# A gated feed-forward layer after linear attention: the last four tiles of w_gate and w_val in blocks 3 to 8 as seven products for eight, and the attention of batches 4 to 7 one to four slots ahead of its old place

## The chip, the cores and the metric

One core of one Trainium2 chip. The metric is device time in microseconds (us); with one core, that core's span is what counts. All runs quoted here are compared with runs of the kernel before on the same chip.

## The reference, cut to what matters

```python
# 8 batches, 8 heads, 576 tokens, head size 64
kv  = einsum('bhsd,bhse->bhde', k, v)
o   = einsum('bhsd,bhde->bhse', q, kv)
o   = o / sqrt(mean(o * o, axis=-1) + 1e-6) * g_norm
x   = o.transpose(0, 2, 1, 3).reshape(4608, 512)
g   = x @ w_gate                       # 512 x 1536
val = x @ w_val                        # 512 x 1536
ffn = (gelu(g) * val) @ w_out          # 1536 x 512
out = x + sigmoid(x @ w_res) * ffn
```

The 4,608 tokens go through in nine blocks of 512, numbered 0 to 8. Blocks 0 to 7 hold the first 512 tokens of batches 0 to 7. Block 8 holds the 64 last tokens ("the remainder") of all eight batches. While the layer runs for block m, the attention of batch m+1 is computed between its tiles.

## The kernel before

A block has slots: 12 tiles of w_gate and w_val (128 hidden units each), then the residual gate, then the product with w_out. A tile costs TensorE (PE) eight matmuls of 512 columns. ScalarE (ACT) takes the gelu and VectorE (DVE) multiplies it by the value, which frees the value's PSUM bank:

```python
pmoe  = tile_pool(name="pmoe",  bufs=4, space=PSUM)     # four banks, tag "mm"
pattn = tile_pool(name="pattn", bufs=4, space=PSUM)     # four banks, tag "at"
# ... cut ...
def m_act(blk, f, gps, vps):
    ge = moep.tile([P, NJ * P], FP16, tag="ge", name="ge")
    nc.scalar.activation(out=ge, in_=gps, func=AF.Gelu)
    nc.vector.tensor_tensor(out=hids[blk][:, f, :], in0=ge, in1=vps, op=ALU.mult)   # "hid"

def m_gval(blk, f, pool=pmoe, tag="mm"):
    # ... cut ...
    gps = pool.tile([P, NJ * P], FP32, tag=tag, name="gps")
    m_mm(gps, wg_c, f, blk, 0, NJ)
    vps = pool.tile([P, NJ * P], FP32, tag=tag, name="vps")
    m_mm(vps, wv_c, f, blk, 0, NJ)
    m_act(blk, f, gps, vps)
```

The attention of the next batch is spread over the slots. Its output "op" fills four "at" banks. ACT squares them, DVE sums the squares ("ss"), DVE works out 1/rms (the norm, 12 small operations), and DVE scales the output ("t"). After that t is multiplied by g ("t-times-g") and transposed by DMA into xT, the next block's input:

```python
def plan_attn(b):
    rem = pair(b) is not None            # batches 2, 3, 5, 7 carry remainder rows
    m = b - 1
    # ... b == 2 cut ...
    at(m - 1, NF, lambda: by_token(b, "q"))                  # NF = 12
    at(m - 1, NF + 1, lambda: by_token(b, "k"), *begin)      # begin: q's transposes by DMA
    k0, o0, n0 = 1, 3, 7
    at(m, k0, lambda: a_kv(b))                               # k-times-v
    if rem:
        at(m, o0 - 1, lambda: a_rem_o(b))                    # remainder's output, "orp"
        at(m, o0 + 2, lambda: a_ss(b, NJ))
    at(m, o0, lambda: a_o(b))                                # attention output, "op"
    for j in range(NJ):
        at(m, o0 + j // 2, lambda j=j: a_ss(b, j))           # sums of squares
    at(m, n0, lambda: a_norm(b, 0, NJ + rem))                # the norm
    n0 += 1 if b == 2 else 2
    for j in range(NJ):
        at(m, ..., lambda j=j: a_t(b, j))                    # scalings "t", slots 9 and 10
    for j in range(NJ):
        at(m, ..., lambda j=j: a_x(b, j))                    # t-times-g
    at(m, NF, lambda: d_xT(b, 0, NJ))                        # the transpose into xT
```

The product with w_out is already computed as seven products for eight in blocks 1 to 8 (the Strassen-Winograd scheme). Four sums of quarters of hid ("hid_s", DVE) feed it, and the operation "wF" frees a bank that it needs soon after its start.

## Time and profile before

| | before |
|---|---|
| time | 344.26 us, median of three runs (344.17 to 344.53) |
| busy | PE 96%, DVE 68%, ACT 43%, GpSimd (POOL) 30% |
| blocks 3 and 5 / 4 and 6 (with remainder) | 34.88 / 35.24 and 35.23 us |
| blocks 7 / 8 (no attention inside) | 33.35 / 32.11 us |
| waits of PE in blocks 3 to 8 | none |

A block's length is the time from its first gate matmul to that of the next block, in PE's timeline; block 8 is measured to the start of its last product group. Engine shares are averages over the whole span. The profiled run of before took 347.15 us, because v came late in its opening (PE waited 2.5 us). Spans of profiled runs are therefore not compared here; lengths of blocks are.

### The profile page before, as it was taken

Reading aid. Unit: us, or ns where it says so; the run is one execution under the profiler, and the core shown is the slowest. Engines: PE = TensorE matmul, PEld = TensorE weight load, DVE = VectorE, ACT = ScalarE, POOL = GpSimd, SP = SyncE. Lnnn points to the kernel's source line nnn. Section 1 sums busy time; section 2 is a strip of 40 time slices with the busy share of each in tenths; the row PEclk is TensorE's granted clock in tenths of the full one; section 3 lists DMA queues with packets and bytes.
Section 4 is the critical chain, followed back from the end, with each engine's and each line's share of the span. In section 5 each row is a group of like instructions: output and inputs, shape, how many; then the busy total and the mean of one; then the engine's idle time right before and its main releaser. Section 6 shows DMA issues by size and latency. Waiting matters only on the chain.

```text
span 345.4 us, 6165 instructions
## 1 busy us (share of the span) xinstructions
PE 331.9 (96%) x2432; PEld 188.0 (54%) x2432; DVE 236.5 (68%) x446; ACT 150.1 (43%) x265; POOL 103.1 (30%) x121
## 2 busy tenths in 40 slices
PE   8789999999899999999999999999999999999992
PEld 3544454445744475447544764476447644764481
DVE  5665549769859987698578976885688735453643
ACT  3573384274336352535263615361736133623350
POOL 2692161980064108200820083005000600050013
PEclk9899999999999999999999999999999999999997
DMA  7999999669589263966395439744003120030004
GB/s 244 290 178 204 195 204 166 168 95 150 117 108 164 94 123 120 165 60 128 130 167 43 102 114 174 79 92 153 17 0 61 63 76 2 1 121 4 0 2 121
DMA packets 76399, 38.81 MB, mean 112 GB/s; under 512 B 42066, under 2 KB 73810, under 8 KB 76370
## 3 DMA queue, kind: packets, MB, share of 16 engines
q0 software_dynamic: 38752, 17.17, 40.1%
q1 hardware_dynamic: 37184, 20.71, 21.6%
q10 hardware_dynamic: 434, 0.52, 0.5%
q8 instruction: 19, 0.31, 0.4%
q14 instruction: 10, 0.08, 0.1%
HBM read 38.80 MB, written 9.44 MB: 140 GB/s over the span
## 4 chain that ended last, share of the span: by engine, by line
PE 69%; DVE 2%; issue 0%; POOL 0%; POOLq 0%; DVEq 0%
PE gps L336 21%; PE vps L336 20%; PE wA L431 10%; PE rps L356 6%; PE wF L431 3%; PE wD L431 2%; PE w L431 2%; PE wE L431 2%; PE kvp L187 1%; PE op L205 1%; DVE t L282 1%; DVE hid L325 1%; DVE hid_s L404 0%; DVE t L296 0%; POOL osb L526 0%
## 5 line engine op out<-in xcount | busy, mean ns | idle before, releaser
L324 ACT ACTIVATE ge<-gps 128x512 f16<-128x512 f32 x108 | 64.3, 597 | 133.1 <-PE gps L336 127.8
L325 DVE TENSOR_TENSOR hid<-ge,vps 128x512 f16<-128x512 f16 x108 | 73.8, 684 | 63.2 <-PE vps L336 60.8
L336 PE MATMUL vps<-xT,wv 128*128 128x512 f16 x424 | 108.8, 379 | 0.4 <-DVE hid L325 0.4
L336 PE MATMUL gps<-xT,wg 128*128 128x512 f16 x424 | 109.0, 379 | 0.0
L470 POOL TENSOR_TENSOR osb<-osb,t 128x512 f32<-128x512 f32 x28 | 36.1, 1309 | 155.6 <-DVE osb L466 148.6
L336 PEld LDWEIGHTS <-wv 128*128 128x128 f16 x424 | 41.5, 98 | 50.6 <-issue 0.7
L336 PEld LDWEIGHTS <-wg 128*128 128x128 f16 x424 | 40.2, 98 | 45.4 <-issue 0.4
L431 PEld LDWEIGHTS <-hid_s 128*128 128x128 f16 x384 | 37.5, 98 | 6.3 <-issue 1.4
L356 PE MATMUL rps<-wr,xT 128*128 128x512 f16 x144 | 32.7, 379 | 0.0
L431 PEld LDWEIGHTS <-hid 128*128 128x128 f16 x288 | 28.2, 98 | 5.1
L365 ACT ACTIVATE th<-rps 128x512 f32<-128x512 f32 x36 | 21.5, 597 | 19.0 <-PE rps L356 19.0
L356 PEld LDWEIGHTS <-xT 128*128 128x128 f16 x144 | 14.1, 98 | 16.8
L224 DVE TENSOR_REDUCE ss<-sq 128x8 f32<-128x512 f32 x32 | 20.6, 679 | 2.9 <-ACT sq L222 2.7
L431 PE MATMUL wA<-wo_ts,hid_s 128*128 128x256 f16 x168 | 20.6, 273 | 1.2 <-DVE wF L404 1.2
L370 ACT ACTIVATE th<-th 128x512 f32<-128x512 f32 x36 | 19.9, 622 | 0.0
L282 DVE TENSOR_TENSOR t<-op,ny 128x512 f16<-128x512 f32 x28 | 17.9, 682 | 0.1
L222 ACT ACTIVATE sq<-op 128x512 f32<-128x512 f32 x28 | 15.3, 597 | 4.5 <-PE op L205 4.2
L296 DVE TENSOR_TENSOR t<-t,g 128x512 f16<-128x512 f16 x36 | 16.2, 498 | 0.1
L404 DVE TENSOR_TENSOR hid_s<-hid 128x1536 f16<-128x1536 f16 x16 | 15.3, 955 | 0.3
L526 POOL TENSOR_TENSOR osb<-osb,t 128x512 f32<-128x512 f32 (+1 forms) x4 | 4.3, 1078 | 27.8 <-DVE osb L522 27.8
L373 PE MATMUL fps<-wo,hid 128*128 128x512 f16 x48 | 11.2, 379 | 0.0
L431 PE MATMUL wD<-wo_ts,hid_s 128*128 128x256 f16 x84 | 10.3, 273 | 0.1
(133 smaller groups left out, 326.5 us busy)
## 6 DMA issues: line engine op xcount, KB each, us to landing
out_dram<-osb SPq DMA_DIRECT2D x14, 512.0 KB, 2.6
qraw<-in_q_dram POOLq DMA_DIRECT2D x7, 512.0 KB, 8.2
kraw<-in_k_dram POOLq DMA_DIRECT2D x7, 512.0 KB, 9.9
v<-in_v_dram POOLq DMA_DIRECT2D x7, 512.0 KB, 11.9
out_dram<-osb SPq DMA_DIRECT2D x5, 256.0 KB, 2.8
wg<-in_moe_w_gate_dram POOLq DMA_DIRECT2D x2, 512.0 KB, 9.2
wv<-in_moe_w_val_dram POOLq DMA_DIRECT2D x2, 512.0 KB, 9.4
wo<-in_moe_w_out_dram POOLq DMA_DIRECT2D x2, 512.0 KB, 14.2
```

The costliest lines, as they stand in the source:

```text
L222: nc.scalar.activation(out=sq, in_=src, func=AF.Square)
L224: nc.vector.tensor_reduce(out=out_, in_=sq, op=ALU.add, axis=mybir.AxisListType.X)
L282: nc.vector.tensor_tensor(out=t, in0=o, in1=scale, op=ALU.mult)
L296: nc.vector.tensor_tensor(out=t_t[blk][:, jj, :], in0=t_t[blk][:, jj, :], in1=g16, op=ALU.mult)
L324: nc.scalar.activation(out=ge, in_=gps, func=AF.Gelu)
L325: nc.vector.tensor_tensor(out=hids[blk][:, f, :], in0=ge, in1=vps, op=ALU.mult)
L336: nc.tensor.matmul(ps[:, j0 * P : j1 * P], lhsT=w[:, cc, :], rhs=xT_t[blk][:, j0:j1, cc, :], start=(cc == 0 and j0 == 0), stop=(cc == NP - ...
L356: nc.tensor.matmul(rps, lhsT=xT_t[blk][:, j, cc, :], rhs=wr16[:, cc, :], start=(cc == 0), stop=(cc == NP - 1),)
L365: nc.scalar.activation(out=th, in_=rps, func=AF.Tanh, scale=0.5)
L370: nc.scalar.activation(out=th, in_=th, func=AF.Copy, scale=0.5, bias=0.5)
L431: nc.tensor.matmul(ps[:, e - es[0], :], lhsT=a[:, f, e * P : (e + 1) * P], rhs=b[:, f, :], start=(start and e == es[0] and f == 0), stop=( ...
L470: nc.gpsimd.tensor_tensor(out=res_all[of], in0=res_all[of], in1=t_t[blk][of], op=ALU.add)
```

## The change

The intent is to take columns off PE, which is the busiest engine. For the last four of the 12 tiles in blocks 3 to 8, w_gate and w_val are split into halves of the contraction and of the hidden units, x into halves of the contraction and of the tokens. Seven products of quarters then give what eight did. In exchange there are sums of x (GpSimd), sums of weights (DVE, once), copies (ACT) and additions (DVE). The second part moves the attention of batches 4 to 7 ahead (the output by one slot, the norm by three, the scalings by four), so that it is through DVE before the products begin. Batch 3's attention keeps its slots, but the reordering and transposing of its q and k go later, behind block 1's output.

```diff
+    def gval_by_products(blk):
+        w = [{}, {}]                        # two groups g of 128 hidden units
+        # prod_w: gate and value side by side in one bank, 4 matmuls of 256 columns
+        def first():
+            for g in range(2):
+                w[g]["E"] = pmoe.tile([P, 2, PR], FP32, tag="mm", name="gE")
+                w[g]["D"] = pmoe.tile([P, 2, PR], FP32, tag="mm", name="gD")
+                w[g]["A"] = pattn.tile([P, 2, PR], FP32, tag="at", name="gA")
+                w[g]["d"] = th_all[:, g, :].rearrange("p (n t) -> p n t", n=2)
+                prod_w(w[g]["A"], g, wh(1, 1), x_of(blk, 1, 1), True)
+                nc.scalar.copy(out=w[g]["E"], in_=w[g]["A"])
+            for g in range(2):
+                prod_w(w[g]["D"], g, s_(1), x_sum[:, 0], True)
+                nc.scalar.copy(out=w[g]["d"], in_=w[g]["D"])
+        def second():
+            for g in range(2):
+                prod_w(w[g]["A"], g, s_(2), x_sum[:, 1], False)
+                sub(nc.vector, w[g]["D"], w[g]["A"], w[g]["d"], ALU.add)
+            for g in range(2):
+                prod_w(w[g]["E"], g, wh(1, 2), x_of(blk, 2, 1), False)
+                gelu(g, "C11", w[g]["E"], F0, 0)
+            times(0, "C11")
+        # third(), fourth(): three more products, half gelus and half products; cut
...
             if b == 3:
+                plans[m - 1][NF + 3] = [by_token k, by_token q, *begin] + ...   # behind block 1's output
+            else: # as before
-            k0, o0, n0 = 1, 3, 7
+            k0, o0, n0 = (1, 3, 7) if b == 3 else (0, 2, 4)
...
-        n0 += 1 if b == 2 else 2
+        n0 += 1 if b != 3 else 2                        # scalings in slots 5 and 6
...
-            at(m, NF if b == 2 else n0 + 1, lambda j=j: a_x(b, j))
+            at(m, n0 + 1 if b == 3 else NF, lambda j=j: a_x(b, j))
...
+            plan[10] = [lambda: w_sums(0), lambda: w_sums(1)]       # block 0
...
+            if blk > 2:
+                slots[F0:] = gval_by_products(blk)                  # F0 = 8
+                plan.setdefault(0, []).insert(0, lambda: x_sums(blk))
```

Cut as well: for blocks 3 to 8 the first of the hid sums goes to the end of the tiles beside the other three, and two small buffers change their number. (Three lines of the part on b == 3 are abridged.)

More of the change, by code (lines that the diff above doesn't have):

```diff
@@ L1 @@
 from contextlib import ExitStack
+from functools import partial
 import concourse.bass as bass
@@ L219, in a_ss @@
         o, ss = st[b]["o"][i], st[b]["ss"]
-        sq = attnp.tile([P, 2, NP, D] if i < NJ else [P, H, D], FP32, tag="sq", name="sq")
+        sq = attnp.tile([P, 2, NP, D] if i < NJ else [P, H, D], FP32, tag="sq", bufs=3, name="sq")
         src = o if i < NJ else o.rearrange("p (h d) -> p h d", h=H)
@@ L239, in a_rem_o @@
                     )
-        st[b]["o"][NJ] = o32 = attnp.tile([P, C], FP32, tag="o32", name="o32")
+        st[b]["o"][NJ] = o32 = attnp.tile([P, C], FP32, tag="o32", bufs=1, name="o32")
         for e in range(2):
@@ L438, in prod, with w_of_half, w_sums @@
                 )
+    F0 = NF - 4
+    w_sum = [wpool.tile([P, 4, NP // 2, PR], FP16, name=f"w_sum{i}") for i in range(2)]
+    x_sum = xp.tile([P, 4, NJ // 2, NP // 2, P], FP16, bufs=1, name="x_sum")
+    def w_of_half(n, i, j):
+        return (wg_c, wv_c)[n][-1][:, (j - 1) * 2 : j * 2, (i - 1) * PR : i * PR]
+    def w_sums(n):
+        s_ = w_sum[n]
+        sub(nc.vector, s_[:, 0], w_of_half(n, 2, 1), w_of_half(n, 2, 2), ALU.add)
+        sub(nc.vector, s_[:, 1], s_[:, 0], w_of_half(n, 1, 1))
+        sub(nc.vector, s_[:, 2], w_of_half(n, 1, 1), w_of_half(n, 2, 1))
+        sub(nc.vector, s_[:, 3], w_of_half(n, 1, 2), s_[:, 1])
@@ new lines, in x_of, with x_sums, prod_w, s_ @@
+    def x_of(blk, i, j):
+        return xT_t[blk][:, 2 * (j - 1) : 2 * j, 2 * (i - 1) : 2 * i, :]
+    def x_sums(blk):
+        x_ = partial(x_of, blk)
+        for i, (a, b) in enumerate(
+            [(x_(1, 2), x_(1, 1)), (x_(2, 2), x_sum[:, 0]), (x_(2, 2), x_(1, 2)), (x_(2, 1), x_sum[:, 1])]
+        ):
+            sub(nc.gpsimd, x_sum[:, i], a, b)
+    def gval_by_products(blk):
+        w = [{}, {}]
+        def prod_w(ps, g, a, b, start):
+            for n in range(2):
+                for c in range(NP // 2):
+                    nc.tensor.matmul(
+                        ps[:, n, :],
+                        lhsT=a(n)[:, c, g * P : (g + 1) * P],
+                        rhs=b[:, :, c, :],
+                        start=(start and n == 0 and c == 0),
+                        stop=(c == NP // 2 - 1),
+                        skip_group_check=True,
+                    )
+        def s_(i):
+            return lambda n: w_sum[n][:, i - 1]
+        def wh(i, j):
+            return lambda n: w_of_half(n, i, j)
+        def gelu(g, name, src, f, half):
+            ge = moep.tile([P, PR], FP16, tag="ge", name="ge")
+            nc.scalar.activation(out=ge, in_=src[:, 0, :], func=AF.Gelu)
+            w[g][name] = ge, src, hids[blk][:, f + g, half * PR : (half + 1) * PR]
+        def times(g, name, eng=nc.vector):
+            ge, src, dst = w[g][name]
+            eng.tensor_tensor(out=dst, in0=ge, in1=src[:, 1, :], op=ALU.mult)
+        def first():
[17 more added lines that the diff above has]
+            times(0, "C11")
+        def third():
+            for g in range(2):
+                prod_w(w[g]["A"], g, s_(3), x_sum[:, 2], False)
+                c = res_all[:, g, :].rearrange("p (n t) -> p n t", n=2)
+                sub(nc.vector, c, w[g]["A"], w[g]["d"], ALU.add)
+                gelu(g, "C22", c, F0 + 2, 1)
+                times(g, "C22", nc.gpsimd)
+            times(1, "C11")
+            for g in range(2):
+                prod_w(w[g]["D"], g, s_(4), x_of(blk, 2, 2), False)
+                gelu(g, "C12", w[g]["D"], F0, 1)
+                times(g, "C12")
+        def fourth():
+            for g in range(2):
+                prod_w(w[g]["A"], g, wh(2, 2), x_sum[:, 3], False)
+                gelu(g, "C21", w[g]["A"], F0 + 2, 0)
+                times(g, "C21")
+        return [first, second, third, fourth]
@@ L737, in f_sq @@
     def f_sq(pr, j0, j1):
-        first["sq", pr, j0] = sq = attnp.tile([P, j1 - j0, 2, D], FP32, tag=f"sq{j1 - j0}", name="sq")
+        sq = attnp.tile([P, NJ, 2, D], FP32, tag="sq", bufs=3, name="sq")
+        first["sq", pr, j0] = sq = sq[:, 0 : j1 - j0]
         ps = first["o", pr].rearrange("p j (h d) -> p j h d", h=2)
@@ L909, in plan_attn @@
         else:
-            at(m - 1, NF, lambda: by_token(b, "q"))
-            at(m - 1, NF + 1, lambda: by_token(b, "k"), *begin)
-            k0, o0, n0 = 1, 3, 7
+            if b == 3:
+                plans[m - 1][NF + 3] = [lambda: by_token(b, "k"), lambda: by_token(b, "q"), *begin] + plans[m - 1].get(
+                    NF + 3, []
+                )
+            else:
+                at(m - 1, NF, lambda: by_token(b, "q"))
+                at(m - 1, NF + 1, lambda: by_token(b, "k"), *begin)
+            k0, o0, n0 = (1, 3, 7) if b == 3 else (0, 2, 4)
         at(m, k0, lambda: a_kv(b))
@@ L952 @@
             slots += [lambda i=i: outs[i]() for i in range(4 if blk < B else 2)]
-            plan.setdefault(NFH + 2, []).insert(0, lambda: s_begin(blk))
+            if blk <= 2:
+                plan.setdefault(NFH + 2, []).insert(0, lambda: s_begin(blk))
             def products(blk=blk, outs=outs):
                 s_rest(blk)
+                if blk > 2:
+                    s_begin(blk)
                 outs.extend(out_by_products(blk, blk == 1) if blk < B else out_last(blk))
```

## The prediction

> **What bounds the kernel now.** I read the page's busy line, then the waits of TensorE (PE), then the timelines of PE and VectorE (DVE) through one block. Blocks are the nine groups of 512 tokens, numbered 0 to 8 as in the code; the change touches the last six of them (3 to 8).
>
> ```profile
> span 345.4 us, 6165 instructions
> PE 331.9 (96%) x2432; PEld 188.0 (54%) x2432; DVE 236.5 (68%) x446; ACT 150.1 (43%) x265; POOL 103.1 (30%) x121
> ```
> PE is busy 96% of the span at a granted clock of 0.990, so the bound is PE's instruction stream, unless something makes it wait. The list of what PE waits for:
>
> ```profile
> PE kvp L718 <- DVE v L689: 2.5, 2, 2.3
> PE wA L431 <- DVE wF L404: 1.2, 1, 1.2
> ...
> PE vps L336 <- DVE hid L325: 0.4, 1, 0.4
> ```
> Only the second and third lie after the opening: 1.2 us in block 1 and 0.4 us in block 2. Blocks 3 to 8 have no wait. So taking columns off PE gives time, if nothing else then comes last. What comes nearest is seen in DVE's timeline (start, duration, what) of block 4, which starts at 166.40:
>
> ```profile
> 174.79 0.69 DVE L325 TENSOR_TENSOR hid<-ge,vps 128x512 f16<-128x512 f16 x1 [1.39 <-PE vps L336]
> 175.69 1.28 DVE L224 TENSOR_REDUCE ss<-sq 128x8 f32<-128x512 f32 x2 [0.21 <-ACT sq L222]
> ...
> 182.98 0.18 DVE L254 TENSOR_SCALAR nm<-ss 128x40 f32<-128x40 f32 x1
> ...
> 185.40 0.68 DVE L325 TENSOR_TENSOR hid<-ge,vps 128x512 f16<-128x512 f16 x1
> 186.00 0.95 DVE L404 TENSOR_TENSOR hid_s<-hid 128x1536 f16<-128x1536 f16 x1
> 186.87 0.68 DVE L325 TENSOR_TENSOR hid<-ge,vps 128x512 f16<-128x512 f16 x1
> 187.47 1.28 DVE L282 TENSOR_TENSOR t<-op,ny 128x512 f16<-128x512 f32 x2
> 188.67 0.68 DVE L325 TENSOR_TENSOR hid<-ge,vps 128x512 f16<-128x512 f16 x1
> 189.26 1.28 DVE L282 TENSOR_TENSOR t<-op,ny 128x512 f16<-128x512 f32 x2
> 190.46 1.42 DVE L296 TENSOR_TENSOR t<-t,g 128x512 f16<-128x512 f16 x4
> 191.80 0.68 DVE L325 TENSOR_TENSOR hid<-ge,vps 128x512 f16<-128x512 f16 x1
> ```
> Without brackets there was no idle time: DVE runs unbroken from 182.38 to 197.37, and the gelu-times-value product of the last tile ("hid" at 191.80) comes 2.8 us after PE finished that tile at 189.01. PE doesn't feel it, because the residual-gate matmuls follow. Back to back, a 512-wide DVE operation takes 0.60 us (starts 185.40 to 186.00), four t-times-g 1.34, the norm chain 2.42 (182.98 to 185.40).
>
> **What the Trainium skill says.** "TensorE: Matmul & The Clock Gate", Back-to-back issue gap, gives N/2.4 + 2.5 ns warm: 216 ns for 512 columns, 109 for 256. The trace agrees: four 512-column matmuls every 0.864 us (216 ns each), and twelve 256-column ones every 1.311 us (109.3 ns, line L431), their weight loads hidden. The same page's table of specifications says that VectorE, ScalarE and GpSimd take their queues in strict order; the DVE list above, which follows the program, agrees, and my argument rests on it. "SBUF — State Buffer", Who interferes with whom, says that a DVE instruction with two SBUF inputs blocks against a GpSimd instruction that reads SBUF. It agrees here: one t-times-g takes 0.42 us alone and 1.26 at 203.42, beside GpSimd's additions.
>
> **The change, part by part.**
>
> *Removed and added on PE.* Per block the last four tiles cost 4 x 2 x 4 = 32 matmuls of 512 columns: 32 x 0.216 = 6.91 us. Seven products in two column groups, gate and value, two contraction chunks each, are 7 x 2 x 2 x 2 = 56 matmuls of 256: 56 x 0.1093 = 6.12. Gain 0.79 per block, 4.7 us over six.
>
> *Added beside it.* ScalarE (43% busy): four copies and eight half gelus for four whole ones, about +2.4 us a block. GpSimd (30%): four sums of x, 5.2 us at 1.30 each (the time of its 128x512 f16 row), at the block's head and not needed before tile 8, and two half products. DVE: four 512-wide additions, 2.4 us, and six half-width products (estimate 0.33 each from the 0.43 us of a 256-wide one, less its overlap), 2.0, for the four old ones, 2.4. The weight sums are eight DVE operations of about 0.34 in block 0, where DVE is idle a third of the time: 0.2 us at most.
>
> *Moved.* In blocks 3 to 6, the attention output falls after tile 2 instead of 3, its norm from tile 7 to tile 4, its scalings from tiles 9 and 10 to 5 and 6. So all of it must pass through DVE before the product of tile 7, within the first eight tiles. I laid the queue out by hand for block 4, in us from the block's start. Attention output: 174.62 - 166.40 - 1.73 = 6.49. PE ends tile 7 at 6.49 + 0.57 + 5 x 1.73 = 15.7. First stage: A of both groups to 16.6, D of group 0 to 17.0, D of group 1 wanted at 17.0. DVE: first sum of squares 1.07 after the attention output, as at 175.69: two to 8.8; hid of tile 3 (data 0.27 after PE's 8.8) to 9.7; two sums to 10.9; hid 4 to 11.5; sum of the remainder to 12.1; norm to 14.5; hid 5 to 15.1; two scalings to 16.3; hid 6 to 16.9; two scalings to 18.1; hid 7 to 18.7.
>
> E0, D0, E1 and D1 take all four banks of the "mm" PSUM pool, so one of them needs the bank from which hid 7 reads. PE therefore waits in its first stage until 18.7: **1.75 us**. In blocks 3 and 5 there is no remainder (0.6 less on DVE, 0.08 less norm, 0.34 less on PE before the attention output): hid 7 ends at 17.7, D1 is wanted at 16.65: **1.1 us**. Sum over blocks 3 to 6: 2 x 1.1 + 2 x 1.75 = +5.7 us. Blocks 7 and 8 have no attention, DVE was idle 1.04 us in front of each hid there, and they keep the 0.79.
>
> After the products DVE has four half-hidden sums (4.0), four t-times-g (1.34), two reorderings (1.2) and then wF, which frees PE's next use of wA. In block 4 that ends about 0.3 us late; in blocks 3 to 5 together +0.8. The x transpose is now issued after the t-times-g, and its landing (4.3 us median) I place 1.4 us before the next block wants it.
>
> *Block 1 and 2.* Batch 3's reorderings go behind the block's output work. That takes 1.2 us off DVE in front of wF: -1.0 of the 1.2 us wait. But the q transpose is then issued only about 2.8 us into block 2 (1.6 to issue) and that of the remainder after it (lands 2.6 later), while the remainder's output is wanted after tile 1: +0.6.
>
> Sum: -4.7 + 5.7 + 0.8 - 1.0 + 0.6 + 0.2 = +1.6, so 345.9 by the walk. I take half a microsecond off, since each of the five wait terms may be eaten by slack that I don't see: **345.4 us**.
>
> **Rivals.**
> - *The whole gain arrives*: 344.26 - 4.7 - 1.0 = 338.5. For it: nothing in blocks 3 to 8 waits now, and the author moved attention ahead just to clear DVE. Against: between the first sum of squares and hid 7 lie 11.1 us of DVE work, and PE gives it only 9.4 (7.6 to 17.0). If DVE's order let hid 7 pass before the last scalings, 1.2 us less in four blocks: 341.
> - *The x transpose lands late.* t-times-g now waits behind the hidden sums; if DMA takes 3 us longer, the four blocks 4 to 7 start 1.6 us late each: 352. Against: the DMA share is low at the ends of the blocks and median landing is 4.3.
> - *GpSimd becomes the bound of a product.* Its two products per block read SBUF and could hold up the hidden sums; the batch loads are issued about 5 us later, behind the x sums. Against: loads landed in 8 to 12 us and are next read at about 30 of a block's 35, and GpSimd is empty at tile 9. Worth at most +2: 347.5.
>
> **Range and chances.** Between the rival with the full gain and the one with late transposes, the walk's errors are a few tenths in each of some ten places: 340.0 to 348.5. A gain over 2% (below 337.4) is more than the products give and would need waits that the profile doesn't have: 0.03. Over 2% slower (above 351.1) needs late transposes in each block: 0.03. Within 2%: 0.94.
>
> **What would show it.** Right: blocks 7 and 8 come out 0.8 us shorter than 33.35 and their like; blocks 3 and 5 some 0.3 to 0.6 us longer, 4 and 6 some 1 us longer than 34.9 and 35.3; a wait of PE for hid of 1 to 1.8 us once in each of blocks 3 to 6, at "gD" or "gE"; the 1.2 us wait for wF in block 1 gone; a wait of the remainder's output in block 2 for the transposed q remainder. Wrong: no such wait and all blocks 3 to 8 shorter by 0.8 (then DVE operations overlap more than I counted, or the slot came free earlier), or a wait of the next block's first gate matmul for xT. An error in the banks' order would shift the wait to "gE" or to the first A, without removing it.

## The result, and the profile after

| | before | after | ratio (95%) |
|---|---|---|---|
| time, us | 344.38 (344.17 to 344.53, 4 runs) | 345.43 (345.15 to 345.73, 4 runs) | 1.0031 (1.0014 to 1.0048) |

A ratio is the mean time of one kernel's runs over that of the other's of the same rounds, so it is not quite the ratio of the medians. The change costs 1.05 us, within 2%.

The page of the kernel after, its head and the row of busy times:

```profile
span 343.9 us, 6640 instructions
PE 328.4 (95%) x2576; PEld 200.4 (58%) x2576; DVE 250.8 (73%) x490; ACT 165.4 (48%) x313; POOL 137.5 (40%) x157
```

PE is busy 3.5 us less (331.9 before), and still the time went up. (The products take away more than that, some 4.8 us by blocks 7 and 8; but of the new waits, 6.7 us by the starts of the matmuls, only 4.8 are listed as waits, and the rest counts as busy, because the ends of matmuls are modelled.) Blocks from PE's timelines say where it went (us):

| block | 1 | 2 | 3 | 4 | 5 | 6 | 7 | 8 | sum |
|---|---|---|---|---|---|---|---|---|---|
| before | 36.62 | 36.24 | 34.88 | 35.24 | 34.88 | 35.23 | 33.35 | 32.11 | 278.55 |
| after | 35.42 | 36.58 | 35.38 | 36.62 | 35.40 | 36.34 | 32.55 | 31.26 | 279.55 |
| difference | -1.20 | +0.34 | +0.50 | +1.38 | +0.52 | +1.11 | -0.80 | -0.85 | +1.00 |

Only blocks 7 and 8 keep the gain of the products; blocks 3 to 6, which also hold attention, lose it and more. The sum of +1.00 accounts for the +1.05 that was timed. What PE waits for in the kernel after (total us, times, longest us; a few rows of the opening left out):

```profile
PE gD L476 <- DVE hid L326: 4.5, 4, 1.2
...
PE kvp L820 <- POOL v L791: 0.6, 1, 0.6
PE vps L337 <- DVE hid L326: 0.4, 1, 0.4
PE gA L476 <- DVE t L283: 0.3, 1, 0.3
PE orp L234 <- DMA qrT<-qr: 0.3, 1, 0.3
```

The first row is new: once in each of four blocks, "gD" waits for a gelu-times-value product of DVE. The wait for wF, 1.2 us before, is no longer in the list, and a small one of the remainder's output for its transposed q has come. PE's timeline at the first stage of block 4, which starts at 163.56 (start, duration, what, and the idle time before it in brackets):

```profile
178.41 1.03 PE L337 MATMUL vps<-xT,wv 128*128 128x512 f16 x4
179.70 0.39 PE L476 MATMUL gA<-xT,wg 128*128 128x256 f16 x2 [0.27 <-DVE t L283]
...
180.30 0.39 PE L476 MATMUL gA<-xT,wg 128*128 128x256 f16 x2
...
180.90 0.61 PE L476 MATMUL gD<-x_sum,w_sum 128*128 128x256 f16 x4
182.69 0.60 PE L476 MATMUL gD<-x_sum,w_sum 128*128 128x256 f16 x4 [1.18 <-DVE hid L326]
```

The lines left out are the other matmuls of gA. Four matmuls of 256 columns take 0.44 us (four times 0.1093), so the last line could have started at 180.90 + 0.44 = 181.34: PE lost 1.35 us there. The bracket says 1.18, because it counts from the modelled end of the matmuls before. In the same way gA is 0.43 us late at 179.70 (178.41 + 4 x 0.216 = 179.27 would follow from the tile before), and the second gA, at 180.30, and the first gD are 0.16 late each. DVE in the same stretch:

```profile
171.12 1.28 DVE L225 TENSOR_REDUCE ss<-sq 128x8 f32<-128x512 f32 x2 [0.21 <-ACT sq L223]
...
175.74 0.18 DVE L255 TENSOR_SCALAR nm<-ss 128x40 f32<-128x40 f32 x1
...
178.37 0.68 DVE L326 TENSOR_TENSOR hid<-ge,vps 128x512 f16<-128x512 f16 x1
178.96 1.28 DVE L283 TENSOR_TENSOR t<-op,ny 128x512 f16<-128x512 f32 x2
180.16 0.68 DVE L326 TENSOR_TENSOR hid<-ge,vps 128x512 f16<-128x512 f16 x1
180.75 1.28 DVE L283 TENSOR_TENSOR t<-op,ny 128x512 f16<-128x512 f32 x2
181.95 0.68 DVE L326 TENSOR_TENSOR hid<-ge,vps 128x512 f16<-128x512 f16 x1
183.81 1.30 DVE L405 TENSOR_TENSOR gD<-gA,th 128x512 f32<-128x512 f32 x2 [1.18 <-issue]
...
195.50 0.70 DVE L405 TENSOR_TENSOR wF<-wA,wd 128x512 f32<-128x512 f32 x1
```

The norm, the hid of tile 5, two scalings, the hid of tile 6, two scalings and the hid of tile 7 run one behind the other without a bracket. Tile 7's hid ends at 181.95 + 0.68 = 182.63, and gD starts at 182.69. Right behind it DVE is idle for 1.18 us: it had been the late one, and then has nothing to do until PE has run gD and gA. wF comes late enough to hold PE for 0.07 us only.

### The profile page after: what moved, and what is told of

Read it like the earlier page. It is cut to its first block, busy times and chain, and to the rows that moved or that the text cites. A ratio compares the mean times of both kernels' runs of the same rounds, so it can differ in the third digit from the quotient of the medians.

```text
span 343.9 us, 6640 instructions
## 1 busy us (share of the span) xinstructions
PE 328.4 (95%) x2576; PEld 200.4 (58%) x2576; DVE 250.8 (73%) x490; ACT 165.4 (48%) x313; POOL 137.5 (40%) x157
## 5 line engine op out<-in xcount | busy, mean ns | idle before, releaser
L325 ACT ACTIVATE ge<-gps 128x512 f16<-128x512 f32 x84 | 50.0, 598 | 105.2 <-PE gps L337 100.5
L326 DVE TENSOR_TENSOR hid<-ge,vps 128x512 f16<-128x512 f16 x84 | 57.3, 684 | 44.3 <-PE vps L337 42.1
L337 PE MATMUL vps<-xT,wv 128*128 128x512 f16 x328 | 84.2, 379 | 0.5 <-DVE hid L326 0.4
L337 PE MATMUL gps<-xT,wg 128*128 128x512 f16 x328 | 84.3, 379 | 0.0
L337 PEld LDWEIGHTS <-wv 128*128 128x128 f16 x328 | 32.0, 98 | 39.6 <-issue 0.7
L337 PEld LDWEIGHTS <-wg 128*128 128x128 f16 x328 | 30.8, 98 | 34.1 <-issue 0.4
L498 POOL TENSOR_TENSOR hid<-ge,osb 128x256 f16<-128x256 f16 x12 | 8.0, 674 | 63.7 <-ACT ge L493 63.7
L476 PEld LDWEIGHTS <-w_sum 128*128 128x128 f16 x192 | 18.6, 98 | 7.8 <-issue 5.2
L405 POOL TENSOR_TENSOR x_sum<-xT,x_sum 128x512 f16<-128x512 f16 x12 | 13.9, 1154 | 0.5
```

Source lines behind the costliest of these rows:

```text
L337: nc.tensor.matmul(ps[:, j0 * P : j1 * P], lhsT=w[:, cc, :], rhs=xT_t[blk][:, j0:j1, cc, :], start=(cc == 0 and j0 == 0), stop=(cc == NP - ...
L405: eng.tensor_tensor(out=out_, in0=in0, in1=in1, op=op)
L476: nc.tensor.matmul(ps[:, n, :], lhsT=a(n)[:, c, g * P : (g + 1) * P], rhs=b[:, :, c, :], start=(start and n == 0 and c == 0), stop=(c == N ...
```

## The experiments

Two sets, each on one chip, with three rounds and therefore four runs of each kernel. All eight kernels gave the right result. Their block lengths (us):

| block | 1 | 2 | 3 | 4 | 5 | 6 | 7 | 8 |
|---|---|---|---|---|---|---|---|---|
| e1, gD bank | 35.41 | 36.57 | 34.19 | 35.43 | 34.22 | 35.15 | 32.55 | 31.27 |
| e2, scalings later | 35.41 | 36.54 | 34.18 | 35.41 | 34.19 | 35.14 | 32.55 | 31.26 |
| e3, attention only | 35.41 | 37.41 | 34.88 | 35.24 | 34.88 | 35.23 | 33.35 | 32.11 |
| e4, one slot back | 35.41 | 36.65 | 36.59 | 37.53 | 36.63 | 37.46 | 32.55 | 31.27 |
| e5, e1 and e2 | 35.42 | 36.55 | 34.79 | 36.03 | 34.80 | 35.76 | 32.55 | 31.26 |
| e6, products in 7, 8 | 35.41 | 36.54 | 34.88 | 35.23 | 34.88 | 35.24 | 32.55 | 31.26 |
| e7, e2 and q first | 35.41 | 36.24 | 34.17 | 35.41 | 34.17 | 35.14 | 32.55 | 31.26 |
| e8, e7 and banks | 35.41 | 36.23 | 34.15 | 35.22 | 34.14 | 35.02 | 32.55 | 31.26 |

The theory: PE's wait is one of order. gD of group 1 takes the fourth "mm" bank, which tile 7's hid reads, and DVE comes to that hid only after the scalings. The rivals: DVE has too much work before the products, so that a cure at one place moves the wait to the next; or the products themselves (copies on ACT, products on GpSimd) bring the loss.

### e1: another bank for gD of group 1

```diff
-                w[g]["D"] = pmoe.tile([P, 2, PR], FP32, tag="mm", name="gD")
 ...
             for g in range(2):
+                pool, tag = ((pmoe, "mm"), (pattn, "at"))[g]
+                w[g]["D"] = pool.tile([P, 2, PR], FP32, tag=tag, name="gD")
                 prod_w(w[g]["D"], g, s_(1), x_sum[:, 0], True)
```

> gD of group 1 goes to the attention pool, so no product has to wait for the bank that hid of tile 7 still reads. Theory (the bank held by a late hid 7 costs blocks 3 to 6 their gain): PE's wait of gD for hid, 4.5 us in four places, falls to under 0.4 in all, and the time to about 340.8 us (340.0 to 342.0), 4 to 5 under the changed kernel and about 1% under before. Rival 1 (the second stage waits for its own operands: the x sums on GpSimd or the copies on ScalarE): the wait stays at gD or moves to the next product, time 344.5 to 345.5. Rival 2 (the bank goes free but DVE's queue only hands the wait on, to gA of the third stage, which needs the D sums): half the gain, about 343.

Measured: 341.07 us against 344.82, ratio 0.9919 (0.9855 to 0.9982; one of the four runs took 345.55 and one of before's eight 349.10, which makes the interval wide). PE's timeline in block 3 now has both groups of gD in one unbroken row of eight, without a bracket:

```profile
144.45 1.08 PE L476 MATMUL gD<-x_sum,w_sum 128*128 128x256 f16 x8
```

Nothing of DVE's work was taken away or reordered here. Only the bank differs, and blocks 3 to 6 fall by 1.18 to 1.19 us each. The wait was for that bank.

### e2: the last two scalings behind tile 7

```diff
-  at(m, NF if b == 2 and j > 1 else n0 + j // 2, lambda j=j: a_t(b, j))
+  at(m, NF if b == 2 and j > 1 else n0 + (j // 2) * (2 if b > 3 else 1), lambda j=j: a_t(b, j))
```

> Only the order on DVE changes: the last two scalings of batches 4 to 7 go behind hid 7 instead of in front of it (1.2 us of DVE work). Theory: gD's wait is hid 7's place in DVE's queue, so it shrinks by 1.2 us in each of four blocks: gone in blocks 3 and 5, some 0.2 to 0.4 left in 4 and 6; time about 340.8 us (340.0 to 342.5). Rival 1 (operands of the products): no change, 345.4. Rival 2 (DVE is full and hands the wait on): the D sums come 1.2 us later and PE waits for them at the third stage; time 343 to 345.4.

Measured: 340.96 us against 344.82, ratio 0.9893 (0.9873 to 0.9913). DVE's timeline in block 4:

```profile
177.51 1.28 DVE L283 TENSOR_TENSOR t<-op,ny 128x512 f16<-128x512 f32 x2
178.71 1.27 DVE L326 TENSOR_TENSOR hid<-ge,vps 128x512 f16<-128x512 f16 x2
179.90 1.28 DVE L283 TENSOR_TENSOR t<-op,ny 128x512 f16<-128x512 f32 x2
```

and PE's of the same place:

```profile
179.44 1.19 PE L476 MATMUL gD<-x_sum,w_sum 128*128 128x256 f16 x8
```

The same operations, two of them exchanged with a hid: tile 7's hid is done at 179.98 instead of behind the second pair of scalings, and gD's eight matmuls follow each other, only 0.15 us longer than the 1.04 of an undisturbed eight. Block 4 falls from 36.62 to 35.41. What it still lacks of the full gain (35.24 less 0.79 is 34.45) stands mostly in front of gD: the first gA again comes 0.43 us late, with the first scaling named as the releaser, and the second gA and gD about 0.16 late each. A total shortage of DVE time would not have been cured by an exchange, so the first rival falls as the explanation of this wait. The two cures give the same lengths within 0.03 us in each block, as one and the same wait would.

### e3: the attention moved, without the products

Diff against the kernel after: the lines with gval_by_products, x_sums and w_sums are taken out.

> The moves alone (attention ahead, batch 3's reorderings late, the hidden sum late), without products: last four tiles in eight products as before. Theory: without products hid 7's lateness costs nothing, because tiles 8 and 9 need its bank later; blocks 3 to 6 have no wait, block 1 is 1.2 us shorter, block 2 about 0.3 longer: 343.5 us (343.0 to 344.2). Rival (the move itself delays PE, by later loads or a late x transpose): 345 or more.

Measured: 344.58 us against 344.82, ratio 1.0003 (0.9969 to 1.0037). That is a miss: 0.4 us above the range that I had named. Blocks 3 to 8 are as before to the hundredth, so the move alone costs nothing there. Block 1 gains its 1.21, but block 2 loses 1.17. PE's waits name the reason:

```profile
PE orp L234 <- DMA qrT<-qr: 1.1, 1, 1.1
```

The late transposes of batch 3's q, a part of the same move, ate the gain of block 1. In the kernel after the same wait is only 0.3 us. It is not the products that soften it: up to block 3 the two kernels differ in the weight sums of block 0 alone, and in both the second transpose goes out 3.99 us after the start of block 2 (95.49 - 91.50 and 95.59 - 91.60). Its data was used 3.31 us after that in e3 and 2.47 after it in the kernel after; what made it land later is not known, and each is one profile.

### e4: products with the attention one slot back

```diff
-            k0, o0, n0 = (1, 3, 7) if b == 3 else (0, 2, 4)
+            k0, o0, n0 = (1, 3, 7) if b == 3 else (1, 3, 5)
-   ... n0 + j // 2 ...
+   ... n0 + (j // 2 if b < 4 else 0) ...        # all four scalings in slot 6
```

> A dose: attention of batches 4 to 7 starts one slot later (output after tile 3, norm at tile 5, all four scalings at tile 6), still all in front of hid 7. Theory: one hid leaves the stretch in front (0.6 us) and the start comes 1.73 us later, so hid 7 ends about 1.1 us later and the wait of the first stage grows by that in four blocks, partly at gA, whose bank comes free with the first scaling: 349.9 us (348.5 to 351). Rival (the wait has to do with x sums, copies or contention with GpSimd, which don't move here): 345.4.

Measured: 351.76 us (350.72 to 352.99) against 344.82, ratio 1.0201 (1.0173 to 1.0230), so not certainly over 2%. That too is a miss: 0.8 us above the range that I had named (348.5 to 351). PE's waits:

```profile
PE gA L476 <- DVE t L283: 6.0, 4, 1.8
PE gD L476 <- DVE hid L326: 3.0, 4, 0.7
```

Blocks 3 to 6 are 1.21, 0.91, 1.23 and 1.12 us longer than after, 4.5 us in all, near the 4.4 expected: one slot of attention is worth about a microsecond in each block, and it is paid first at gA, whose "at" bank the scalings free. The blocks add up to 5.5 us over before, while the medians differ by 6.9. Of the remaining 1.4 us, 1.0 is that the profiled run was the fastest of the four (350.72 against a median of 351.76); the other runs were not profiled, so where they lost their time is not known.

A stronger form, with the attention of batches 4 to 7 left entirely in its old place, could not be run: the build itself ends in a deadlock, since gA asks for an "at" bank ahead of the scalings that free it. So some move ahead is a condition of these products.

### e5: both cures together

Diff against the kernel after: the edits of e1 and e2.

> Both cures at once: the last two scalings behind hid 7, and gD of group 1 in the attention pool. Each alone brought about 341. If what counts is which reader holds the bank that a product needs, the two undo each other: gD of group 1 now waits for the bank from which the third scaling reads, and that scaling runs after hid 7. So the wait comes back, named after the scaling: 0.6 to 0.8 us in each of four blocks, time 342.5 to 344 (343.4 by my walk). Rival (each cure works by spreading DVE's load, whatever the bank): 340.5 or less.

Measured: 343.07 us against 344.52, ratio 0.9962 (0.9947 to 0.9977).

```profile
PE gD L476 <- DVE t L283: 2.1, 4, 0.6
```

As expected, the cures spoil each other. Now gD of group 1 takes an "at" bank, which e2's postponed scalings free, and waits half a microsecond for them in each block. That is the theory's sharpest test: against the kernel before, the change stands at +1.05 us, e1 at -3.75, e2 at -3.86 and both together at -1.45 (medians, each against before on its own chip). Two edits worth 4.8 and 4.9 us give 2.5 together, and the releaser's name changes from hid to t.

### e6: products in blocks 7 and 8 only, attention in its old slots

Diff: `blk > 2` becomes `blk > 6` for the products, and the slots of the attention are those of before. Batch 3's late reorderings stay.

> Products only in blocks 7 and 8, which have no attention, the attention of batches 4 to 7 in its old place. Theory: those two blocks keep the whole 0.8 us each and blocks 3 to 6 are as before: block 1 1.2 shorter, block 2 0.3 to 1.2 longer, time 342.3 to 343.3 against 344.8 of before on this chip. If the products cost anything by themselves, it is more.

Measured: 342.09 us against 344.52, ratio 0.9931 (0.9916 to 0.9946), 0.2 below the range expected, which was reckoned from a before of 344.8 where this chip had 344.52; block 2 lost only 0.3, the least that I had allowed for. Blocks 7 and 8 fall by 0.80 and 0.85, blocks 3 to 6 are as before. So products with their copies and GpSimd's share are no loss in themselves, and the second rival falls: the loss needs products and attention in one block.

### e7: e2, with batch 3's q reordered ahead of its k

```diff
-  plans[m - 1][NF + 3] = [by_token k, by_token q, *begin] + ...
+  plans[m - 1][NF + 3] = [by_token q, *begin, by_token k] + ...
```

> The kernel with the last two scalings behind hid 7 (341.0), and batch 3's q reordered before its k, so that its two transposes are issued 0.6 us sooner. Theory: PE's wait of the remainder's output for the transposed q remainder in block 2 (0.2 to 1.1 us in the runs so far) goes, and block 2 falls from 36.55 to 36.25 us; time 340.4 to 340.9. If the transpose is slow for another reason, no change.

Measured: 340.31 us against 344.52, ratio 0.9888 (0.9872 to 0.9905), 0.1 below the range expected. The DMA queue's timeline of the kernel after (start and time to issue):

```profile
93.84 1.65 SPq L301 DMA_TRANSPOSE qT<-q  x1
95.59 1.22 SPq L309 DMA_TRANSPOSE qrT<-qr  x1
```

and of e7:

```profile
92.89 1.63 SPq L301 DMA_TRANSPOSE qT<-q  x1
94.63 1.24 SPq L309 DMA_TRANSPOSE qrT<-qr  x1
```

Both transposes go out 0.95 us earlier, about 0.3 of which is that e7's block 1 began earlier (the transpose of xT before them stands at 86.69 rather than 87.03). Block 2 falls from 36.54 in e2 to 36.24, its length before the change, and PE's wait at "orp" is gone.

### e8: the banks chosen so that both fit

```diff
-                w[g]["E"] = pmoe...; w[g]["D"] = pmoe...; w[g]["A"] = pattn...
+                for n in "AE":
+                    w[g][n] = pmoe.tile([P, 2, PR], FP32, tag="mm", name="g" + n)
 ...          # at the product of D:
+                w[g]["D"] = pattn.tile([P, 2, PR], FP32, tag="at", name="gD")
-   ... n0 + j // 2 ...
+   ... n0 + j // 2 + (b > 3) ...                # scalings in slots 6 and 7; e7's edit of q kept
```

> As the one before, but the first products take the banks that come free first: gA from the mm pool (bank of value tile 5 and gate tile 7), gD from the attention pool; scalings behind hid 6 and hid 7. Theory: blocks 4 and 6, which still took 35.4 and 35.15 us (0.79 under before would be 34.45), fall to 34.7 to 34.9; blocks 3 and 5 stay at 34.2; time 339.3 to 340.2. Rival (there DVE is short of time in all, whatever the banks): 340.7 and a wait for the D or C sums in the second or third stage.

Measured: 339.96 us against 344.52, ratio 0.9869 (0.9854 to 0.9884). Blocks 3 and 5 are at 34.15 and 34.14, and 34.88 less the products' 0.79 is 34.09: almost nothing is left there. Blocks 4 and 6 missed what I expected (34.7 to 34.9): they took 35.22 and 35.02, where 35.24 - 0.79 is 34.45.

```profile
PE gA L476 <- ACT gE L507: 0.4, 2, 0.2
```

In block 4 PE loses 0.24 us at gD, 0.45 around the second gA, where the copy by ACT is named, and 0.10 in the third stage. The copy is itself late, and not for want of time on ACT. DVE and ACT in block 4, and the same copy in block 3:

```profile
178.93 0.67 DVE L326 TENSOR_TENSOR hid<-ge,vps 128x512 f16<-128x512 f16 x1
...
179.69 0.57 ACT L507 COPY gE<-gA 128x512 f32<-128x512 f32 x1 [1.05 <-PE gD L476]
...
144.32 0.57 ACT L507 COPY gE<-gA 128x512 f32<-128x512 f32 x1 [0.17 <-DVE hid L326]
```

With this order of banks the copy for group 1 writes the bank that tile 7's hid reads. That hid ends at 178.93 + 0.67 = 179.60, and the copy starts 0.09 us behind it after ACT had stood idle for 1.05; in blocks 3 and 6 it starts 0.10 behind hid 7. In block 3 the profile names hid; in block 4 it names gD, which the copy neither reads nor writes. So the bank that hid 7 holds is still what PE waits for, now by way of the copy. In the blocks with a remainder the rival about too much work on DVE holds in part: hid 7 comes late even with two scalings behind it, and the edit moved the wait. All in all 0.77 us are left in block 4 and 0.57 in block 6. I made no experiment that takes this rest apart.

## Why the prediction was right

The time was predicted at 345.4 us and came out at 345.43. Part of that closeness is luck: the walk's sum was 345.9, I took half a microsecond off for slack, and errors of terms cancelled.

| term of the sum | predicted | measured | from |
|---|---|---|---|
| products, six blocks | -4.7 | 0.80 and 0.85 in blocks 7 and 8; with 0.80 in each of the others, -4.85 | blocks 7, 8 |
| waits in the first stage, blocks 3 to 6 | +5.7 | +6.5 | gaps in PE's timeline: 1.22, 2.10, 1.25 and 1.90 |
| late wF | +0.8 | +0.2 | gaps at wA in the same blocks |
| wait for wF in block 1 | -1.0 | -1.2 | block 1 |
| remainder's q in block 2 | +0.6 | +0.3 | block 2 |
| weight sums | +0.2 | +0.03 | block 0, 34.68 to 34.71 |
| sum | +1.6 (345.9) | +1.0 | blocks: +1.0 |

- **What bounds it, and the mechanism of the loss.** Right. The wait stands once in each of blocks 3 to 6, at gD, with hid named, and e1 and e2 each remove it. The step "E0, D0, E1 and D1 take all four banks of the "mm" PSUM pool, so one of them needs the bank from which hid 7 reads" is what e1 tests.
- **The queue laid out by hand.** The first sum of squares was put at 7.56 us into block 4 (6.49 + 1.07) and came at 171.12 - 163.56 = 7.56. Tile 7's end on PE was put at 15.7 and came at 179.27 - 163.56 = 15.71. The hid of tile 7 was put at 18.7 and ended at 19.07: the norm chain took 178.37 - 175.74 = 2.63 us where I had taken 2.42 from before, it began 0.08 later than I had it, and the last hid counts 0.68 to its end and not 0.60. So the wait was mis-sized by 0.35 in block 4 and by 0.1 to 0.15 in the other three. The prediction's own figures would have made the miss larger: it laid out 18.7 - 17.0 = 1.7 and 17.7 - 16.65 = 1.05, and entered 1.75 and 1.1, so its walk should have summed to +1.4 and not +1.6.
- **A wait not named.** A part of the loss in blocks 4 and 6 comes ahead of that wait (0.75 us in block 4, 0.43 of it at the first gA, where a scaling is named as the releaser: it frees an "at" bank). It shifts PE, so that less is left to wait at gD; the end is set by hid 7 all the same.
- **wF.** Mis-sized: +0.8 predicted for blocks 3 to 5, 0.2 measured. The next use of wA comes only about 0.07 us late in each (block 4: its product starts at 196.25, where 194.87 + 1.31 = 196.18 would follow). In e2, which has no wait at gD, it is the same 0.07, so the two terms don't hide each other. The term that was too large is the hid sums: I had taken 4.0 us for the four, and DVE went through them in 192.96 - 189.24 = 3.72.
- **The rivals.** The full gain did not arrive, and most of it came only when the order or the bank was changed (e1, e2; the best version, e8, is at -4.6 where the rival had -5.7). The 341 that I named for "if DVE's order let hid 7 pass before the last scalings" is e2's 340.96. The transposes of x did not land late: the median landing was the 4.3 us of before, and no wait of the next block's gate matmuls for xT is in the list. GpSimd did not bind: no wait of PE names it in blocks 3 to 8, and its sums of x, at 1.15 us each where I had estimated 1.30, were done at 171.56 in block 4, 9 us before gD reads them.

## What to carry to other kernels

When columns are taken off the busiest engine, ask at once which buffer the shorter stage asks for next, who reads it last, and what stands in front of that reader in its engine's queue. Here 4.8 us of matmuls were saved and lost again, most of it to two scalings in front of one product, and exchanging them with it on DVE, or one bank of PSUM, brought most of it back. Apply such cures one at a time: of two good ones, each worth 4.8 us or more, both together brought only 2.5, because one took a bank that the other made late.

## What the Trainium skill lacked or had wrong

- "TensorE: Matmul & The Clock Gate", Back-to-back issue gap, gives a sustained spacing of about 131 ns for 512-column matmuls with their weight loads, and says that its formula N/2.4 + 2.5 counts too much there. Here a dense stream with a weight load for each matmul had 216 ns for 512 columns (0.864 us for four) and 109.3 for 256 (1.311 us for twelve), which is the formula and not the sustained figure.
- "VectorE: DVE Perf Modes", The TRN2 errata, gives (N+151)/0.96 ns for one addition, 691 ns at N = 512. The duration agrees (0.67 to 0.70 us in the rows of one 512-wide addition or product here), but operations that follow without a wait start 0.60 us apart (two in 1.28). A queue added up from the durations would come out about 15% too long. This section does not say so; "Vector Engine (DVE) Microarchitecture Reference", Measured stream behaviour on trn2, has 1.0417 ns per column plus about 75 ns after queue overlap, from which I estimate 608 ns.
- None of the pages looked up says how to estimate when a PSUM bank comes free if its reader stands in a queue behind other work. Here moving two operations of 0.60 us behind that reader was worth 4.9 us in a kernel of 345 (e2), 1.2 in each of four blocks.
